# First transform with the matrix stationary, and its layout changed over HBM (FFT filter and top-1 mixture of experts, one core)

## The chip, the core and the metric

The program runs on one core of a Trainium2 chip. TensorE (PE) multiplies matrices and writes to PSUM, VectorE (DVE) and ScalarE (ACT) work element by element, GpSimd (POOL) does a part of that and issues indirect transfers, and SyncE (SP) issues the other DMA transfers; each engine executes its own instructions in the order in which the program put them there. The metric is the device time of one execution in microseconds, as the median of several.

## The reference: what is computed

```python
X = np.fft.rfft(x, axis=1)                    # x: 8 sequences x 2496 x 256
Y = X * (filt_r + 1j * filt_i)[None, :, :]
y = np.fft.irfft(Y, n=2496, axis=1)           # then 19968 rows of 256
expert_idx = np.argmax(y @ w_gate, axis=1)    # 8 experts
gate_w = softmax(y @ w_gate)[row, expert_idx]
out[row] = gate_w * (relu(y[row] @ w1[e]) @ w2[e])    # 256 -> 1024 -> 256
```

All of it is float32. The filter runs along the 2496 positions of a sequence, for each of 256 channels apart.

## The kernel before, in words

A sequence of 2496 positions is seen as 39 x 64 (position = 64 n1 + n2). The first transform goes along n1 (39 values become 39 real numbers: one constant, 19 cosines, 19 sines), the second along n2, with the twiddle factors in its matrices `bm`. Then come the product with the filter, the inverse along n2 (`cm`) into the tiles `U`, and the inverse along n1 (`dm`) together with the routing.

A *unit* u is one sequence and one half of its channels (128 of 256): 16 units. A unit has 5 *steps*, one for each group of four bins k, so t = 0 to 79. What a step t does, in the names of the functions:

- `forward1(u, j)`, six times for a unit: for up to four groups of three n2, the data `x` (117 rows of three n2 and 39 n1, 128 channels) are the stationary operand and the block matrix `a1` the moving one. The result in PSUM has channels on partitions; ACT, for one j DVE, copies it into `T` (lines 255 and 263).
- `spec1(t)`: four transposes of `T` (line 295) bring n2 to the partitions, and ACT copies the result to `z` (line 301).
- `spec2(t)`: eight products with `bm` (line 313); `filt_` and `join` (lines 330, 343 and 344) multiply by the filter and join the parts on DVE and POOL; `spec3(t)`: four products with `cm` (line 355), and ACT copies to `U` (line 360).

Beside the steps run the inverse of a sequence that is finished (`inv1` to `inv3`: transposes on line 622, products on line 648, copies on 629, 634 and 650, rows scattered to HBM by POOL on line 158), the routing (`route1` to `route6`) and the preparation of the experts' weights (`w_load` to `w_out`). All of these are put in one list with a key that is counted in steps, and the list is sorted by the key; this gives the order on every engine. From key 78 on the blocks of 128 rows go through the experts (lines 1030 and 1056); most of them run after the last step.

SP issues all plain transfers in the order of the list. A transfer that waits (for a free buffer, say) holds back what stands behind it on SP.

Of the kernel before, what the change touches and what calls it, by code (L numbers as in the profile page):

```python
# [22 lines left out]
N1, N2 = 39, 64  # L23
# [4 lines left out]
GP = 3 * N1  # L28
DUP = 18
# [9 lines left out]
def _dft_tables():  # L39
    n1, n2 = np.arange(N1), np.arange(N2)  # L40
    a = np.zeros((N1, N1))
# [72 lines left out]
def tile_fft_moe(ctx, tc, x, filt_r, filt_i, w_gate, w1, w2, cst, out):  # L114
# [22 lines left out]
    wscr = dram.tile([E, 128, 8256], F16, name="wscr")  # L137

# [46 lines left out]
    with ExitStack() as fctx:  # L185
# [3 lines left out]
        xp = pool(name="xp", bufs=3)  # L189
        up = pool(name="up", bufs=1)  # L190
        tp = pool(name="tp", bufs=1)
# [8 lines left out]
        sp = early(name="sp", bufs=2)  # L200
        pY = early(name="pY", bufs=3, space=PSUM)
# [4 lines left out]
        T = [tp.tile([128, N1, N2], F32, name=f"T{i}") for i in range(2)]  # L206
        a1 = fp.tile([GP, GP], F32, name="a1")
# [20 lines left out]
        xt = {}  # L228

        def loadx(u, c):  # L230
            b, h = divmod(u, 2)
            xv = x[b].rearrange("(n1 n2) d -> n1 n2 d", n2=N2)[
                :, :, h * 128 : (h + 1) * 128
            ]
            t = xp.tile([GP, 4, 128], F32, name=f"x{u}_{c}", tag="x", bufs=4)
            g0, g1 = BANKS[c]
            for l in range(3):
                n = min(g1, NG if l == 0 else NG - 1) - g0
                s0 = 3 * g0 + l
                nc.sync.dma_start(  # L240
                    t[l * N1 : (l + 1) * N1, :n, :],
                    xv[:, s0 : s0 + 3 * (n - 1) + 1 : 3, :],
                )
            for g in range(g0, g1):
                xt[u, g] = t[:, g - g0, :]

        BANKS = ((0, 4), (4, 8), (8, 12), (12, 16), (16, 20), (20, 22))

        def forward1(u, j):
            g0, g1 = BANKS[j]  # L250
            n = 0
            ps = pY.tile([128, 512], F32, name=f"f1_{u}_{j}", tag="pY")
            for g in range(g0, g1):
                m = GP if g < NG - 1 else N1
                nc.tensor.matmul(  # L255
                    ps[:, n : n + m],
                    lhsT=xt.pop((u, g))[:m],
                    rhs=a1[:m, :m],
                    start=True,
                    stop=True,  # L260
                )
                n += m
            (nc.scalar.copy if j in (0, 1, 2, 3, 5) else nc.vector.tensor_copy)(  # L263
                T[u % 2].rearrange("p r n -> p n r")[:, 3 * g0 : 3 * g0 + n // N1, :],
                ps[:, :n].rearrange("p (n r) -> p n r", r=N1),
            )
# [23 lines left out]
        def spec1(t):  # L290
            u, it = divmod(t, 5)
            ps = pA.tile([128, 4, 128], F32, name=f"pt{t}", tag="pF")
            for kk in range(4):
                o = max(0, 2 * (4 * it + kk) - 1) * 64
                nc.tensor.transpose(
                    ps[:, kk],
                    T[u % 2].rearrange("p r n -> p (r n)")[:, o : o + 128],
                    ident,
                )
            z = wp.tile([128, 4, 128], F32, name=f"z{t}", tag="z")  # L300
            nc.scalar.copy(z, ps)  # L301
            stk[t] = z

        def spec2(t):
            u, it = divmod(t, 5)
            z = stk[t]

            ps = pB.tile([128, 2, 2, 128], F32, name=f"px{t}", tag="pF")
            for j in range(2):
                for i in range(2):  # L310
                    for a in range(2):
# [4 lines left out]
                            rhs=z[:, kk],  # L316
# [5 lines left out]
        def filt_(t):  # L322
            u, it = divmod(t, 5)
            h = u % 2
# [22 lines left out]
        def spec3(t):  # L347
            u, it = divmod(t, 5)
# [3 lines left out]
            for kk in range(4):  # L352
# [8 lines left out]
                U[u % NU].rearrange("p n r -> p r n")[:, r0 : r0 + o // 64, :],  # L361
                ps[:, :o].rearrange("p (r n) -> p r n", n=N2),
# [390 lines left out]
        nc.gpsimd.dma_start(ident, cst["ident"])  # L753
        loadk(bm, "bm", 0, 1, nc.gpsimd)
        loadx(0, 0)
        loadx(0, 1)
        loadf(0)
        loadx(0, 2)
        loadx(0, 3)
        loadk(bm, "bm", 1, 2)  # L760
        loadk(cm, "cm", 0, 1)
# [6 lines left out]
        for j in range(6):  # L768
            forward1(0, j)
            if j < 2:  # L770
                loadx(0, j + 4)
# [50 lines left out]
        slow = lambda t: min(1.0, max(0.6, 1.0 - 0.06 * (t - 72)))  # L822
        for t in range(NT):
            u, it = divmod(t, 5)
            rho = slow(t)
            at(t, spec1, t)
# [4 lines left out]
            if 0 < t < 5:  # L831
                at(max(t - 1.8, 0.05), loadf, t)
            if u + 1 < NU_ALL and it == 0:
                for j in range(6):
                    at(t + K["f"] + K["fd"] * j if u else 1.6 + 0.55 * j, forward1, u + 1, j)
            if u + 1 < NU_ALL and it == 0:
                for j in range(6):

                    n = 6 * (u + 1) + j - 4
                    v, i = divmod(n, 6)  # L840
                    z = 5 * (v - 1) + K["f"] + K["fd"] * i + 0.02
                    if v < 2:
                        z = 1.6 + 0.55 * i + 0.02 if v else 0.2 + 0.25 * j
# [340 lines left out]
```

## Time and profile before

| | us |
|---|---|
| median of 3 executions (1471.96 to 1482.54) | 1473.03 |
| the profiled execution | 1473.7 |
| its span, first to last instruction | 1471.9 |

```profile
PE 1345.9 (91%) x15559; PEld 1207.6 (82%) x15559; DVE 879.7 (60%) x2550; ACT 846.7 (58%) x1440; POOL 485.7 (33%) x525
```

This is the first part of the profile's page: for each engine its busy time, the share of the span, and the instructions. PEld are the weight loads of TensorE, which overlap with its products. A share over the whole span is a mean over stages of different kinds: some 81 us of start, six sequences in a steady rhythm, the last steps, the last inverse and routing, and then the experts alone.

### The profile page before, as it was taken

How to read it: one execution, taken by the hardware profiler on the slowest of the kernel's cores; microseconds unless marked ns; L12 is line 12 of the kernel's file. 1: busy time of each engine (PE TensorE's matmuls, PEld its weight loads, DVE VectorE, ACT ScalarE, POOL GpSimd, SP SyncE). 2: the span in 40 equal slices, each digit the busy share in tenths (PEclk: the TensorE clock that was granted, in tenths of full speed). 3: DMA queues.
4: the chain of work that ended last, by engine and by line, in shares of the span. 5: the costliest groups of instructions: out<-in, count | busy, mean ns of one | idle time of the engine just before them, and what ended most of it. 6: DMA issues, size and time to landing. Idle time of an engine off the chain costs nothing.

```text
span 1471.9 us, 41507 instructions
## 1 busy us (share of the span) xinstructions
PE 1345.9 (91%) x15559; PEld 1207.6 (82%) x15559; DVE 879.7 (60%) x2550; ACT 846.7 (58%) x1440; POOL 485.7 (33%) x525
## 2 busy tenths in 40 slices
PE   6888888889989878689999999999999999999997
PEld 5767677777867667479999988999998998999997
DVE  1589788797987657245555554555555555555552
ACT  2547566566755455356666655665566565665564
POOL 1235665656656652432111111111111111111111
PEclk7899999999998999799999999999999999999999
DMA  5744544545543252249346369534535336434631
GB/s 165 210 154 158 163 145 162 176 157 176 165 143 98 73 179 59 84 127 271 73 107 163 81 154 338 158 78 106 155 77 155 104 77 174 91 77 105 157 75 44
DMA packets 200119, 199.18 MB, mean 135 GB/s; under 512 B 104707, under 2 KB 178100, under 8 KB 191724
## 3 DMA queue, kind: packets, MB, share of 16 engines
q1 hardware_dynamic: 180396, 153.80, 37.2%
q0 software_dynamic: 19520, 42.71, 10.4%
q8 instruction: 124, 2.03, 0.6%
q14 instruction: 79, 0.65, 0.1%
HBM read 347.54 MB, written 61.56 MB: 278 GB/s over the span
## 4 chain that ended last, share of the span: by engine, by line
PE 46%; DMA 4%; issue 2%; DVE 2%; SPq 1%; ACT 1%; POOL 0%; POOLq 0%; ACTq 0%; DVEq 0%
PE ph L1030 24%; PE po L1056 22%; DMA wa<-wscr 2%; DMA wb<-wscr 2%; DVE hl L1044 1%; SPq L939 1%; ACT hs L1036 0%; ACT hh L1038 0%; POOL out_dram L158 0%; DMA xt<-xs 0%; SPq L1017 0%; DVE m L995 0%; ACT xs L1009 0%; SPq L947 0%; SPq L977 0%
## 5 line engine op out<-in xcount | busy, mean ns | idle before, releaser
L1030 PE MATMUL ph<-xt,wa 128*128 128x128 f16 x7728 | 468.5, 221 | 24.8 <-DMA wa<-wscr 12.5
L1030 PEld LDWEIGHTS <-wa 128*128 128x128 f16 x7728 | 450.3, 99 | 37.3 <-issue 17.4
L1044 DVE TENSOR_TENSOR hl<-hs,hh 128x512 f16<-128x512 f32 x322 | 223.1, 693 | 376.0 <-ACT hh L1038 319.0
L1056 PE MATMUL po<-wb,hh 128*128 128x256 f16 x2576 | 432.9, 273 | 4.4 <-DMA wb<-wscr 2.1
L158 POOL DMA_INDIRECT out_dram<-ot,t x161 | 158.7, 986 | 693.9 <-DVE xs L1010 616.7
L1056 PE MATMUL po<-wb,hl 128*128 128x256 f16 x1288 | 351.6, 273 | 0.5 <-issue 0.4
L1056 PEld LDWEIGHTS <-hh 128*128 128x128 f16 x2576 | 245.4, 98 | 34.9 <-issue 5.8
L1036 ACT ACTIVATE hs<-ph 128x512 f32<-128x512 f32 x322 | 191.9, 596 | 108.6 <-PE ph L1030 98.3
L158 POOL DMA_INDIRECT xs<-yt,dest x176 | 184.4, 1048 | 132.1 <-issue 65.3
L1009 ACT ACTIVATE xs<-xb,s 128x256 f16<-128x256 f32 x161 | 82.0, 509 | 228.2 <-DVE s L999 226.7
L1038 ACT CAST hh<-hs 128x512 f16<-128x512 f32 x322 | 199.5, 620 | 10.3
L1056 PEld LDWEIGHTS <-hl 128*128 128x128 f16 x1288 | 126.2, 98 | 15.9 <-issue 1.1
L255 PE MATMUL f<-a,x 117*128 117x117 f32 x704 | 108.1, 298 | 16.8 <-DMA x<-in_x_dram 15.1
L360 ACT COPY U<-pi 128x512 f32<-128x512 f32 (+1 forms) x80 | 88.0, 1099 | 58.7 <-PE pi L355 56.4
L255 PEld LDWEIGHTS f<-a,x 117*128 117x128 f32 x704 | 98.2, 211 | 25.0 <-issue 16.0
L1010 DVE SCALAR_TENSOR_TENSOR xs<-xb,s,xs 128x256 f16<-128x256 f32 x161 | 78.3, 486 | 55.7 <-ACT xs L1009 52.9
L343 POOL TENSOR_TENSOR p<-tr,ti 64x256 f32<-64x256 f32 x80 | 65.4, 818 | 137.3 <-DVE ti L330 123.1
L355 PE MATMUL pi<-cm,p 128*128 128x128 f32 (+1 forms) x640 | 92.7, 289 | 11.6 <-POOL p L344 7.7
L355 PEld LDWEIGHTS pi<-cm,p 128*128 128x128 f32 x640 | 81.3, 197 | 22.4 <-issue 11.5
L263 ACT COPY T<-f 128x468 f32<-128x468 f32 (+1 forms) x80 | 71.2, 890 | 46.9 <-PE f L255 45.7
L313 PE MATMUL px<-z,bm 128*64 128x128 f32 x1280 | 92.5, 289 | 3.7 <-ACT z L301 2.1
L650 ACT COPY yt<-py 117x512 f32<-117x512 f32 x88 | 53.0, 603 | 61.4 <-PE py L648 34.8
(171 smaller groups left out, 1488.2 us busy)
## 6 DMA issues: line engine op xcount, KB each, us to landing
wb<-wscr SPq DMA_DIRECT2D x134, 1040.0 KB
wa<-wscr SPq DMA_DIRECT2D x134, 1024.0 KB
xb<-xs SPq DMA_DIRECT2D x161, 130.0 KB
x<-in_x_dram SPq DMA_DIRECT2D x240, 78.0 KB
wf<-in_moe_w_dram SPq DMA_DIRECT2D x32, 512.0 KB
wscr<-wh SPq DMA_DIRECT2D x8, 1040.0 KB
wscr<-wh SPq DMA_DIRECT2D x8, 1024.0 KB
xs<-yt,dest POOLq DMA_INDIRECT x176
```

The lines of the kernel that those rows point to most:

```text
L158: nc.gpsimd.indirect_dma_start(out=dst, out_offset=bass.IndirectOffsetOnAxis(ap=idx, axis=0), in_=src, in_offset=None, bounds_check=bound, ...
L255: nc.tensor.matmul(ps[:, n : n + m], lhsT=xt.pop((u, g))[:m], rhs=a1[:m, :m], start=True, stop=True,)
L313: nc.tensor.matmul(ps[64 * a : 64 * a + 64, i, j], lhsT=bm[:, 4 * it + kk, 64 * i : 64 * i + 64], rhs=z[:, kk], start=True, stop=True,)
L355: nc.tensor.matmul(ps[:, o : o + n], lhsT=p[:, kk], rhs=cm[:, k, :n], start=True, stop=True)
L360: nc.scalar.copy(U[u % NU].rearrange("p n r -> p r n")[:, r0 : r0 + o // 64, :], ps[:, :o].rearrange("p (r n) -> p r n", n=N2),)
L1009: nc.scalar.activation(xs_[:, 0], xb[:, :D], AF.Copy, scale=sc)
L1010: nc.vector.scalar_tensor_tensor(xs_[:, 1], xb[:, :D], sc, xs_[:, 0], op0=ALU.mult, op1=ALU.subtract)
L1030: nc.tensor.matmul(ps[:, f], lhsT=w[:, p : p + 128], rhs=xt[:, r, c], start=(n == 0), stop=(n == 5))
L1036: nc.scalar.activation(s, ps, AF.Relu, scale=1.0 / B23)
L1038: nc.scalar.copy(hh, s)
L1044: nc.vector.tensor_tensor(hl, s, hh, op=ALU.subtract)
L1056: nc.tensor.matmul(ps, lhsT=h2[q][:, f % 4], rhs=wv[:, r, f], start=(f == 0 and n == 0), stop=(f == 7 and n == 2),)
```

## The change: what it does

- The matrix `a1` is now the stationary operand of the first transform (117 x 120: three n2 at once, 40 rows for each, cosines ahead of sines) and the data the moving one, with two groups and all 256 channels at a time: 512 columns. There are 11 products for a sequence in place of 44, and 11 copies (ACT) into `y`.
- `y` goes to HBM (`fscr`), six transfers for a sequence, and comes back as `z` with n2 on the partitions: 30 transfers for a sequence, six for each group of bins. The transposes, `T` and the copies to `z` are gone.
- `x` is loaded for all 256 channels at once. The two halves of the channels take turns in the steps: t now counts sequence, group of bins, half. `z`, `bm` and the filter's group `ff` so serve two steps in a row.
- The copy to `U` writes runs of eight adjacent elements and reads PSUM with a stride; before it read adjacent elements and wrote with a stride.

```diff
-    a = np.zeros((N1, N1))
+    a = np.zeros((N1, 40))
-        a[:, 2 * k - 1], a[:, 2 * k] = np.cos(ph), -np.sin(ph)
+        a[:, k], a[:, 20 + k] = np.cos(ph), -np.sin(ph)
...
+    fscr = [dram.tile([FR, NG, D], F32, name=f"fscr{i}") for i in range(2)]
...
+        def loadx(b, c):
+            xv = x[b].rearrange("(n1 n2) d -> n1 n2 d", n2=N2)
+            t = xp.tile([GP, 4, D], F32, name=f"x{b}_{c}", tag="x")
+            n = min(4, NG - 4 * c)
+            for l in range(3 if n == 4 else 2):
+                o = NG * l + 4 * c
+                nc.sync.dma_start(
+                    t[l * N1 : (l + 1) * N1, :n, :], xv[:, o : o + n, :]
+                )
...
+        def forward1(b, j):
+            c, i = divmod(j, 2)
+            m, q = (GP, FR) if j < 10 else (2 * N1, 80)
+            ps = pY.tile([128, 512], F32, name=f"f1_{b}_{j}", tag="pY")
+            nc.tensor.matmul(
+                ps[:q],
+                lhsT=a1[:m, :q],
+                rhs=xt[b, c][:m, 2 * i : 2 * i + 2, :].rearrange("p g d -> p (g d)"),
...
+                yt1[b, c] = xp.tile([FR, 4, D], F32, name=f"y{b}_{c}", tag="y", bufs=2)
...
+                nc.sync.dma_start(fscr[b % 2][:q, 4 * c : 4 * c + n, :], y[:q, :n, :])
...
+        def loadz(b, it):
+            z = wp.tile([128, 4, D], F32, name=f"z{b}_{it}", tag="z", bufs=4)
             for l in range(3):
...
+                n = NG if l < 2 else N2 - 2 * NG
+                for a in range(2):
+                    o = 40 * l + 20 * a + 4 * it
+                    nc.sync.dma_start(
+                        z[64 * a + NG * l : 64 * a + NG * l + n],
+                        fscr[b % 2][o : o + 4, :n, :].rearrange("k g d -> g k d"),
+                    )
...
-                            rhs=z[:, kk],
+                            rhs=z[:, kk, h * 128 : h * 128 + 128],
...
-                U[u % NU].rearrange("p n r -> p r n")[:, r0 : r0 + o // 64, :],
-                ps[:, :o].rearrange("p (r n) -> p r n", n=N2),
+                U[u % NU][:, :, r0 : r0 + o // 64],
+                ps[:, :o].rearrange("p (r n) -> p n r", n=N2),
...
+        f1 = lambda b, j: 10 * (b - 1) + (0.3 + 0.6 * j if b > 1 else 1.5 + 0.5 * j)
```

Three places show how the order moves. The first is TensorE in the steady part, a stretch of about a step and a half: before, `pt` are the transposes, `f` the first transform, `px` and `pi` the products with `bm` and `cm`.

```order
L295 MATMUL pt_1877<-ident,T_108 128x128 x4
L313 MATMUL px_1889<-z_1803,bm 64x128 x8
L255 MATMUL f_6_2_1903<-a_109,x_2_1634 128x117 x4
L355 MATMUL pi_1913<-cm,p_1793 128x128 x4
L622 MATMUL pg_1_1919<-ident,U_123 117x128
...
L295 MATMUL pt_1936<-ident,T_108 128x128 x4
```

```order
L246 MATMUL f_3_3_1380<-x_1_878,a_106 120x512
L313 MATMUL px_1392<-z_0_1005,bm 64x128 x8
...
L354 MATMUL pi_1421<-cm,p_1294 128x128 x4
L621 MATMUL pg_9_1427<-ident,U_118 117x128
...
L246 MATMUL f_3_4_1450<-x_2_950,a_106 120x512
```

The transposes are gone, and single products of 512 columns stand where groups of four products of 117 columns stood.

The second is SP in the steady part, of the change alone; `fscr<-y` are the writes, `z<-fscr` the loads back, `wf` and `wscr` the experts' weights.

```order
L261 DMA fscr_59<-y_4_913 120x1024
L237 DMA x_2_950<-in_x_dram 39x1024 x3
L261 DMA fscr_59<-y_5_982 80x512
L237 DMA x_3_986<-in_x_dram 39x1024 x3
L271 DMA z_0_1005<-fscr_59 22x4x256 x4
L271 DMA z_0_1005<-fscr_59 20x4x256 x2
L271 DMA z_1_1012<-fscr_59 22x4x256 x4
L271 DMA z_1_1012<-fscr_59 20x4x256 x2
L470 DMA wscr<-wh_0_955 128x4096
```

Between the loads of `x` now stand the writes of `y`, and the first load of `z` stands behind the last write of its sequence, for which it waits.

The third is SP at the start, before and now.

```order
L240 DMA x_0_133<-in_x_dram 39x4x128 x3
L240 DMA x_1_137<-in_x_dram 39x4x128 x3
L280 DMA ff_125<-in_filt_r_dram 32x512
...
L286 DMA ff_125<-in_filt_i_dram 32x2x256
L240 DMA x_2_153<-in_x_dram 39x4x128 x3
L240 DMA x_3_157<-in_x_dram 39x4x128 x3
```

```order
L237 DMA x_3_140<-in_x_dram 39x1024 x3
...
L261 DMA fscr_59<-y_4_196 120x1024
L261 DMA fscr_59<-y_5_204 80x512
L271 DMA z_0_207<-fscr_59 22x4x256 x4
...
L271 DMA z_1_214<-fscr_59 20x4x256 x2
L289 DMA ff_122<-in_filt_r_dram 32x512
```

The filter's first group (`ff`) moved from behind the second load of `x` to behind all writes of the first sequence and two groups of loads of `z`.

## Rows read from the trace of the kernel before

**Rows 1.** Busy time in five stretches: from the start to the product with `bm` of step 10, six sequences of steps (10 to 69), the last ten steps, the last inverse and routing, the experts alone. Columns: stretch, its length, busy us of PE, PEld, DVE, ACT, POOL (instructions), granted TensorE clock as a share of 2.4 GHz, busy share of the 16 DMA engines, GB/s.

```profile
0.00:81.30 81.30, 58.64 (x433) 50.47 (x433) 35.70 (x59) 31.62 (x40) 17.80 (x30) 0.83 0.66 190
81.30:465.90 384.60, 341.95 (x2954) 284.61 (x2954) 323.68 (x697) 240.74 (x351) 226.94 (x246) 0.96 0.49 156
465.90:532.50 66.60, 52.27 (x431) 40.92 (x430) 40.56 (x104) 33.82 (x57) 47.98 (x54) 0.97 0.41 137
532.50:640.00 107.50, 85.81 (x881) 70.90 (x881) 50.46 (x193) 48.46 (x88) 39.35 (x42) 0.85 0.25 68
640.00:1472.00 832.00, 807.26 (x10866) 760.72 (x10863) 429.28 (x1498) 492.10 (x905) 153.64 (x156) 0.99 0.50 129
```

**Rows 2.** The timeline of TensorE where the products with `bm` of steps 0, 10, 70 and 79 begin (start, us, engine, line, operation).

```profile
21.93 1.66 PE L313 MATMUL px<-z,bm 128*64 128x128 f32 x16
...
81.32 0.48 PE L313 MATMUL px<-z,bm 128*64 128x128 f32 x2
...
465.90 0.33 PE L313 MATMUL px<-z,bm 128*64 128x128 f32 x2
...
532.51 0.48 PE L313 MATMUL px<-z,bm 128*64 128x128 f32 x2
```

**Rows 3.** The stretch of the six sequences again, for one line each: in this order line 255 (first transform; PE, PEld), line 295 (transposes; PE, PEld), line 263 (copies to `T`; DVE, ACT), line 301 (copies to `z`; ACT). Then line 255 and line 295 in the last ten steps.

```profile
81.30:465.90 384.60, 77.59 (x528) 70.48 (x528) 0.96 0.49 156
...
81.30:465.90 384.60, 39.54 (x241) 30.00 (x240) 0.96 0.49 156
...
81.30:465.90 384.60, 11.65 (x12) 53.67 (x60) 0.96 0.49 156
...
81.30:465.90 384.60, 35.35 (x60) 0.96 0.49 156
...
465.90:532.50 66.60, 3.96 (x28) 3.51 (x28) 0.97 0.41 137
...
465.90:532.50 66.60, 5.08 (x32) 3.53 (x32) 0.97 0.41 137
```

**Rows 4.** Groups of instructions by line and shape in the same 384.6 us: busy us, mean ns of one, idle time before them and what ended it. A plain float32 product is two instructions here.

```profile
L313 PE MATMUL px<-z,bm 128*64 128x128 f32 x960 | 67.9, 285 | 1.6 <-ACT z L301 1.2 <-DVE gq L634 0.4
...
L648 PE MATMUL py<-gh,dlo 117*117 117x512 f32 x61 | 24.8, 407 | 0.0
...
L486 PE MATMUL plw<-U,wg 128*32 128x351 f32 x192 | 18.5, 480 | 14.3 <-DVE gl L516 7.2 <-ACT U L360 6.3 <-issue 0.8
...
L360 ACT COPY U<-pi 128x512 f32<-128x512 f32 x48 | 54.0, 1125 | 24.9 <-PE pi L355 24.1 <-issue 0.7
...
L650 ACT COPY yt<-py 117x512 f32<-117x512 f32 x61 | 36.9, 605 | 39.2 <-PE py L648 30.2 <-PE pg L622 6.4 <-issue 1.2
...
L301 ACT COPY z<-pt 128x512 f32<-128x512 f32 x60 | 35.4, 589 | 7.9 <-PE pt L295 7.4
```

**Rows 5.** Who waited for whom in the same stretch (us in total, times, longest), of DVE and of SP's queue.

```profile
DVE tr L330 <- PE px L313: 16.9, 8, 3.6
...
DVE T L263 <- PE f L255: 9.8, 5, 4.1
...
SPq L240 <- PE f L255: 201.1, 53, 8.4
```

**Rows 6.** DMA queues in the same stretch: packets, MB, share of 16 engines' time.

```profile
q1 hardware_dynamic: 44044, 45.43, 36.7%
q0 software_dynamic: 7552, 13.97, 11.8%
```

**Rows 7.** Two shorter stretches, with the columns of rows 1: the one with the highest busy share of DVE, and one with the highest share of the DMA engines (the experts' weights begin to be loaded there).

```profile
100.00:150.00 50.00, 45.77 (x412) 39.57 (x411) 48.20 (x98) 34.42 (x49) 25.30 (x29) 1.00 0.49 157
...
650.00:700.00 50.00, 49.42 (x676) 46.65 (x674) 28.60 (x105) 30.44 (x58) 9.33 (x9) 1.00 0.93 248
```

**Rows 8.** The start: SP's issue of transfers of the filter's group, one of several alike, and the first product with the filter on DVE, which waited for that group.

```profile
19.17 0.42 SPq L280 DMA_DIRECT2D ff<-in_filt_i_dram  x1
...
23.64 0.69 DVE L330 TENSOR_TENSOR tr<-px,ff 128x512 f32<-128x512 f32 x1 [3.71 <-DMA ff<-in_filt_r_dram]
```

More of the change, by code (lines that the diff above doesn't have):

```diff
@@ L28 @@
 GP = 3 * N1
+FR = 120
 DUP = 18
@@ L205, in tile_fft_moe @@
         bm = kp.tile([128, 20, 128], F32, name="bm")
-        T = [tp.tile([128, N1, N2], F32, name=f"T{i}") for i in range(2)]
-        a1 = fp.tile([GP, GP], F32, name="a1")
+        a1 = fp.tile([GP, FR], F32, name="a1")
         dm = fp.tile([GP, GP], F32, name="dm")
@@ L247, in tile_fft_moe @@
[L247 to L266, printed above, removed]
+        yt1 = {}
@@ new lines, in loadx @@
+        def loadx(b, c):
[7 more added lines that the diff above has]
+                )
+            xt[b, c] = t
+        def forward1(b, j):
[6 more added lines that the diff above has]
+                rhs=xt[b, c][:m, 2 * i : 2 * i + 2, :].rearrange("p g d -> p (g d)"),
+                start=True,
+                stop=True,
+            )
+            if i == 0:
+                yt1[b, c] = xp.tile([FR, 4, D], F32, name=f"y{b}_{c}", tag="y", bufs=2)
+            y = yt1[b, c]
+            nc.scalar.copy(
+                y[:q, 2 * i : 2 * i + 2, :].rearrange("p g d -> p (g d)"), ps[:q]
+            )
+            if i == 1 or j == 10:
+                n = 2 * i + 2
+                nc.sync.dma_start(fscr[b % 2][:q, 4 * c : 4 * c + n, :], y[:q, :n, :])
@@ L288, in loadf, with place @@
                         )
[L290 to L302, printed above, removed]
+        def place(t):
+            b, k = divmod(t, 10)
+            it, h = divmod(k, 2)
+            return b, 2 * b + h, it, h
         def spec2(t):
-            u, it = divmod(t, 5)
-            z = stk[t]
+            b, u, it, h = place(t)
+            z = zt[b, it]
             ps = pB.tile([128, 2, 2, 128], F32, name=f"px{t}", tag="pF")
@@ L322, in filt_ @@
         def filt_(t):
-            u, it = divmod(t, 5)
-            h = u % 2
+            b, u, it, h = place(t)
             ps = stk[t]
@@ L347, in spec3 @@
         def spec3(t):
-            u, it = divmod(t, 5)
+            b, u, it, h = place(t)
             p = stk.pop(t)
@@ L752, in tile_fft_moe @@
         nc.gpsimd.dma_start(a1, cst["a1"])
-        nc.gpsimd.dma_start(ident, cst["ident"])
+        for c in range(4):
+            loadx(0, c)
         loadk(bm, "bm", 0, 1, nc.gpsimd)
[L755 to L761, printed above, removed]
         warm = wp.tile([128, 512], BF16, name="warm", tag="lw", bufs=1)
@@ L767, in tile_fft_moe @@
             nc.tensor.matmul(ps, lhsT=warm[:, :128], rhs=warm, start=True, stop=True)
-        for j in range(6):
+        for j in range(11):
             forward1(0, j)
-            if j < 2:
-                loadx(0, j + 4)
+            if j in (1, 3):
+                loadx(0, 4 + j // 2)
+        for it in range(2):
+            loadz(0, it)
+        loadf(0)
+        loadk(cm, "cm", 0, 1)
+        loadk(bm, "bm", 1, 2)
+        nc.gpsimd.dma_start(ident, cst["ident"])
         late = (dm, "dm"), (small, "small"), (zrow, "zrow"), (ids, "ids"), (dup, "dup")
```

55 lines of the change are left out of this document (21 added, 34 removed).

## The prediction

> **What bounds the kernel now.** I read the view of busy time in stretches first, then the timeline for the pace, then the groups by line inside the stretch that the change touches. The stretches [rows 1] show that the last 832 us are the experts alone, with TensorE busy 97%; the change touches nothing there. What the change can win lies ahead of 532.5 us. The products of steps 10 and 70 begin at 81.32 and 465.90 us [rows 2]: six sequences in 384.6 us, 64.1 us each. In these TensorE is busy 341.95 us (0.89), DVE 323.68 (0.84), ACT 240.74, POOL 226.94, and the DMA engines have a share of 0.49. So TensorE is nearest to its limit, and DVE stands close behind it. SP waited 201.1 us for the first transform to free a tile of `x` [rows 5]: transfers run ahead of the products, not behind them. In the waits DVE lost 16.9 us to the products with `bm` and 9.8 us to the first transform [rows 5]. The reader should see a chain of engines in fixed order, in which TensorE leads and DVE would be the next to lead.
>
> **The change part by part, for one sequence (a sixth of the 384.6 us).**
>
> *TensorE, off.* The first transform took 77.59 us and the transposes 39.54 [rows 3]: 12.9 and 6.6 us for a sequence.
>
> *TensorE, on.* 11 products of 512 float32 columns, two instructions each. No row has this shape, so I bound it. A column costs the difference between an instruction of 351 columns (480 ns) and one of 128 (285 ns) [rows 4], over 223 columns: 0.87 ns, so 448 ns for 512 columns, 0.90 us for a product and 9.9 us for 11. From below: an instruction of 512 columns of the inverse took 407 ns [rows 4], so 9.0 us. From above: the present transform's 77.59 us over 528 instructions of 117 columns [rows 3] is 147 ns, or 644 ns for 512 columns, 14.2 us. I take 9.9, because the rows that it comes from differ in columns and the high end includes a new stationary operand for every product, and that is what goes away. TensorE then has 57.0 - 12.9 - 6.6 + 9.9 = 47.4 us.
>
> *DVE.* It loses the copies to `T`: 11.65 us over six [rows 3], 1.9 for one. 53.9 becomes 52.0 us. DVE is now the fullest engine.
>
> *ACT.* Off: 53.67 and 35.35 us [rows 3], 14.8 for one. On: 11 copies at 605 ns (a 512-column copy out of PSUM [rows 4]), 6.7 us. The copy to `U` costs 1125 ns between 589, if the stride of its writes was the whole price, and 1125 if the stride of reads costs as much [rows 4]. Either way ACT falls from 40.1 to between 27 and 32 us for a sequence and is hidden behind DVE; I count nothing for it.
>
> *Transfers.* `y` is 5 x 120 x 4 KB and 80 x 2 KB, 2.62 MB; `z` is 5 x 128 x 4 KB, 2.62 MB. Now 59.4 MB took 48.5% of 384.6 us on all DMA engines [rows 6], 3.14 us for a MB. The 5.24 MB added cost 16.5 us, so the engines are busy 31.1 + 16.5 = 47.6 us for a sequence, still less than DVE. The packets of `x` grow from 512 bytes to 4 KB; what this saves I leave out. SP issues 17 + 6 + 30 transfers for `x`, `y` and `z` in place of 32, 21 more at 0.42 us [rows 8], 8.8 us in time that it now spends waiting [rows 5]. Each new wait on SP (a write for its copy, a load of `z` for the last write or for a free buffer) stands in key order; the loads of `z` are issued some five steps ahead of their use, nearly 30 us, and four tiles of `x` are as far ahead. So in the steady part these waits are covered; if the DMA engines became full that cover would be gone, which is the second rival.
>
> *The steady part.* DVE's 52.0 us set the period if waits allow. TensorE reached 0.89 in this stretch [rows 1], DVE reached 48.20 of 50 us, 0.96, at its fullest [rows 7]. I take 0.92, between the two, since the wait for the first transform is gone and TensorE, which feeds DVE, now has 4.6 us less to do than DVE. 52.0 / 0.92 = 56.5 us. Six sequences: 384.6 - 339 = **46 us saved**. Ends: 0.96 gives 54.2 and 59 us saved, 0.89 gives 58.4 and 34.
>
> *The last ten steps.* TensorE loses 4.0 + 5.1 us [rows 3] of 52.27, POOL keeps its 47.98 of 66.60 [rows 1]. No engine is full, so I take about half, **5 us saved**, between 0 and 9.
>
> *The start.* Up to step 10 the DMA engines are busy 0.66 of 81.3 us [rows 1], 53.7 us. Added by then are `y` of two sequences and `z` of the first and the first group of the second: 8.4 MB, 26.4 us. Together 80.1 us: at a share of 0.93, as in the fullest stretch shown [rows 7], 86 us, and at 0.89, 90. I take **9 us lost**. Besides, the first product with `bm`, at 21.93 us now [rows 2], needs the whole sequence transformed, written and read back, and the filter's group comes after that (12 issues of 0.42 us; DVE waited for that group already now, 3.71 us [rows 8]). Against it, a group of `ff` is now needed every second step. Ends: nothing lost, if the engines fill their gaps, and 20 us, if the round trip and the late filter stand in series with the steps.
>
> *The sum.* -46 - 5 + 9 = -42 us. The last inverse and the experts keep their time. The profiled execution took 1473.7 us with a span of 1471.9, the median is 1473.03; the difference is small, and I take the sum from the median: **1431 us**. The ends together: 1473 - 59 - 9 + 0 = 1405 and 1473 - 34 - 0 + 20 = 1459.
>
> **A rule against the change.** The trace gives one share for all 16 DMA engines, so 47.6 us is a mean. By it the transfers stay behind DVE. The Trainium skill, page "DMA: Bandwidth & Descriptors", section "Why a DMA increments its semaphore by 16 and not by 1", says that a transfer runs on as many engines, at most 16, as divide the outermost sizes of both sides, and on the lowest-numbered ones when SP issues it. By that rule, as an estimate, the loads of `z` with 22 and 20 rows would use 11 and 10 engines, those of `x` 13, the writes of `y` 15; the ten lowest would be busy 54.1 us for a sequence. No row of this case shows single engines.
>
> **The rivals.**
>
> *The transfers bind on a part of the engines.* If the added 2.62 MB of `z` lie on ten or eleven engines, each of these gets 12 of 128 rows, 0.246 MB at 50.2 us for a MB on one engine: 12.3 us; `y` adds 8.8 and the present `x` already lies 1.9 us above the mean: 31.1 + 12.3 + 8.8 + 1.9 = 54.1 us. This exceeds DVE's 52.0; at 0.92 the period is 58.8, 32 us saved: -32 - 5 + 9, **1445 us**. For it: small loads of 22 rows. Against: 512-byte packets of `x` go away. The rule above would give this case. Chance 0.18.
>
> *The transfers bind outright, and it gets slower.* If such a mix of transfers holds only a share of 0.70 (0.66 was reached at the start, while the steps waited for loads [rows 1]), the period is 47.6 / 0.70 = 68.0, 23 us lost over six, and the start takes 80.1 / 0.70 = 114, 33 lost: 23 + 33 - 5, **1524 us**. It decides as soon as the share that can be held falls below 47.6 / 64.1 = 0.74. Against it: 0.93 was held for 50 us [rows 7], with long packets. Chance 0.12.
>
> *The order, not TensorE, makes the rhythm.* If the fixed order keeps DVE at its present 0.84, the period is 52.0 / 0.842 = 61.8, 14 us saved, none at the end: -14 + 9, **1468 us**, no change that counts. For it: the keys were spaced for other costs, and the granted clock could fall with a less busy TensorE (0.96 in this stretch at a busy share of 0.89, 0.85 in 532.5 to 640 at 0.80 [rows 1]). Against: the largest wait of SP and one of DVE's end in the first transform [rows 5]. Chance 0.14.
>
> That the change does not do what it says is ruled out by the order that was shown: no transpose stands between `f` and `px`.
>
> **How the numbers follow.** The forecast of 1431 has the remaining 0.56, with 1405 to 1459 as its own range. The range of 1404 to 1474 takes in the first and third rival and leaves out the slower one, and a little on either side of the ends. About 1% is what a measurement of this kernel can tell from no change: 1458 and 1488. Faster: 0.54 of the forecast, 0.15 of the first rival, 0.01 of the third: 0.70. Within 1%: 0.02, 0.03 and 0.12: 0.17. Slower: 0.12 and 0.01: 0.13.
>
> **What would show it.** In the changed profile: the 11 products for a sequence at 9 to 10 us; DVE at 0.9 or more and TensorE near 0.84 between steps 10 and 70; a distance of 56 to 57 us between sequences; step 10 at about 90 us; a DMA share near 0.84. DVE below 0.87 with loads of `z` or `x` as releasers would speak for the first two rivals, with PE, ACT and DVE releasing each other for the third. The prediction is wrong if the experts' part changes its length, or if the start loses more than the steady part gains.

## The result and the profile after

The changed kernel took 1483.46 us in the median of 20 executions (1478.02 to 1490.86), the kernel before beside it 1473.72 (20 executions). The ratio is 1.0068, 95% interval 1.0051 to 1.0085: slower by 0.7%, where 1431 us and faster were forecast. The profiled execution took 1483.0 us with a span of 1481.2.

The same five stretches as in [rows 1], cut at the products with `bm` of steps 10, 70 and 79, with the same columns:

```profile
0.00:118.30 118.30, 55.97 (x287) 30.47 (x287) 33.42 (x56) 21.31 (x36) 18.07 (x30) 0.73 0.75 212
118.30:478.30 360.00, 314.64 (x2316) 221.05 (x2315) 311.83 (x682) 176.28 (x295) 219.15 (x241) 0.94 0.81 252
478.30:544.20 65.90, 48.18 (x371) 36.21 (x370) 42.59 (x108) 23.76 (x45) 52.90 (x59) 0.92 0.47 157
544.20:650.00 105.80, 83.94 (x867) 69.76 (x867) 49.68 (x193) 47.20 (x88) 38.36 (x40) 0.85 0.25 69
650.00:1481.00 831.00, 807.42 (x10880) 760.49 (x10877) 429.16 (x1498) 490.88 (x905) 154.24 (x157) 1.00 0.51 129
```

| stretch | before | after | difference | forecast |
|---|---|---|---|---|
| start, to step 10 | 81.3 | 118.3 | +37.0 | +9 |
| six sequences | 384.6 | 360.0 | -24.6 | -46 |
| last ten steps | 66.6 | 65.9 | -0.7 | -5 |
| all behind them | 939.4 | 937.0 | -2.4 | 0 |

The sum is +9.3 us. The start took more than the steady part gave. A sequence takes 60.0 us in place of 64.1; DVE works 311.83 / 6 = 52.0 us of it, TensorE 52.4.

The new product, line 246, in the same stretch alone (PE, PEld, clock, DMA share, GB/s):

```profile
118.30:478.30 360.00, 69.77 (x128) 19.23 (x128) 0.94 0.81 252
```

Groups by form in that stretch, which answer to [rows 4]: products with `bm`, copies to `y`, copies to `U`:

```profile
L313 PE MATMUL px<-z,bm 128*64 128x128 f32 x962 | 72.9, 298 | 9.4 <-issue 5.6 <-ACT U L359 3.7
...
L256 ACT COPY y<-f 120x512 f32<-120x512 f32 x58 | 34.0, 586 | 45.4 <-PE f L246 38.2 <-issue 4.4 <-PE px L313 1.7
...
L359 ACT COPY U<-pi 128x512 f32<-128x512 f32 x48 | 29.9, 624 | 58.3 <-PE pi L354 44.4 <-issue 10.4 <-PE f L246 2.5
```

The product takes 69.77 / 128 = 545 ns of TensorE for an instruction, a copy to `y` 586 ns. The copy to `U` fell from 1125 to 624 ns.

Who waited for whom in the start, up to step 10 (us in total, times, longest):

```profile
DVE tr L329 <- DMA ff<-in_filt_r_dram: 35.7, 1, 35.7
ACT y L256 <- DMA fscr<-y: 26.1, 6, 10.6
PE f L246 <- DMA x<-in_x_dram: 23.4, 3, 18.6
DVE wm L387 <- DMA wf<-in_moe_w_dram: 13.1, 3, 10.8
PE px L313 <- DMA z<-fscr: 10.1, 1, 10.1
```

Five different kinds of transfer are waited for. The first wait runs from the beginning, since DVE has no work before it; only some 3 us of it lie behind the first product with `bm`, which was done at 33.7 us while DVE began at 36.86. The same view for the six sequences, DVE and PE:

```profile
DVE tr L329 <- PE px L313: 19.1, 6, 4.4
DVE wh L458 <- ACT wh L453: 9.5, 11, 2.1
...
PE py L647 <- DVE gq L633: 10.9, 10, 2.1
PE pw L410 <- DVE wm L398: 9.7, 7, 2.7
```

No transfer stands among them (in the whole stretch PE and DVE never wait for one by this view, ACT for 1.0 us): the engines wait for each other. The timeline shows how, here at 250 us (the routing comes once in a sequence; TensorE, then DVE):

```profile
248.71 0.49 PE L503 MATMUL pgl<-ident,lw 128*117 128x128 f32 x3
249.04 1.02 PE L246 MATMUL f<-x,a 117*120 117x512 f32 x2
250.90 1.39 PE L485 MATMUL plw<-U,wg 128*32 128x351 f32 x16 [0.84 <-DVE gq L633]
252.22 0.70 PE L621 MATMUL pg<-ident,U 128*117 128x128 f32 x4
252.84 1.09 PE L313 MATMUL px<-z,bm 128*64 128x128 f32 x16
```

```profile
250.46 0.23 DVE L508 COPY gl<-pgl 117x72 f32<-117x72 f32 x1
250.60 0.15 DVE L515 COPY gl<-pgl 117x8 f32<-117x8 f32 x1
254.06 0.69 DVE L329 TENSOR_TENSOR tr<-px,ff 128x512 f32<-128x512 f32 x1 [3.30 <-PE px L313]
```

The routing has one PSUM buffer (`pD`). Its second group of products, `plw`, cannot begin before DVE has copied the first (`gl`, until 250.75; the view names `gq`, which DVE had done by 250.47), and `px` of the next step stands behind `plw` on TensorE. So DVE, having worked off its list, waits 3.30 us for `px`.

The start on TensorE (idle time before, and what ended it, in brackets):

```profile
31.77 1.97 PE L313 MATMUL px<-z,bm 128*64 128x128 f32 x16 [10.09 <-DMA z<-fscr]
52.36 3.46 PE L246 MATMUL f<-x,a 117*120 117x512 f32 x4 [18.62 <-DMA x<-in_x_dram]
70.15 2.06 PE L246 MATMUL f<-x,a 117*120 117x512 f32 x2 [4.60 <-ACT y L256]
82.29 2.06 PE L246 MATMUL f<-x,a 117*120 117x512 f32 x2 [5.33 <-ACT y L256]
117.75 0.59 PE L410 MATMUL pw<-ident,wm 128*1 128x128 f32 x2 [13.82 <-DVE wm L398]
118.27 1.97 PE L313 MATMUL px<-z,bm 128*64 128x128 f32 x16
```

### The profile page after: what moved, and what is told of

Its sections match the earlier page's. It is cut to its first block, busy times and chain, and to the rows that moved or that the text cites. A ratio compares the mean times of both kernels' runs of the same rounds, so it can differ in the third digit from the quotient of the medians.

```text
span 1481.2 us, 39900 instructions
## 1 busy us (share of the span) xinstructions
PE 1310.2 (88%) x14711; PEld 1118.0 (75%) x14711; DVE 866.7 (59%) x2534; ACT 759.4 (51%) x1368; POOL 482.7 (33%) x525
## 4 chain that ended last, share of the span: by engine, by line
PE 45%; DMA 5%; SPq 2%; issue 2%; DVE 1%; ACT 1%; POOL 0%; POOLq 0%; ACTq 0%; DVEq 0%
PE ph L1029 23%; PE po L1055 22%; DMA wb<-wscr 2%; DMA wa<-wscr 2%; SPq L938 1%; SPq L1016 1%; DVE hl L1043 1%; POOL out_dram L160 0%; DMA xt<-xs 0%; SPq L976 0%; ACT xs L1008 0%; ACT hs L1035 0%; SPq L946 0%; ACT hh L1037 0%; DVE xs L1009 0%
## 5 line engine op out<-in xcount | busy, mean ns | idle before, releaser
L246 PE MATMUL f<-x,a 117*120 117x512 f32 (+1 forms) x176 | 100.0, 662 | 39.4 <-DMA x<-in_x_dram 23.4
L313 PE MATMUL px<-z,bm 128*64 128x128 f32 x1280 | 99.2, 303 | 21.4 <-DMA z<-fscr 10.1
L256 ACT COPY y<-f 120x512 f32<-120x512 f32 (+1 forms) x88 | 51.3, 586 | 129.5 <-PE f L246 87.2
L313 PEld LDWEIGHTS px<-z,bm 128*64 128x64 f32 x1280 | 77.7, 150 | 52.7 <-issue 36.4
L354 PEld LDWEIGHTS pi<-cm,p 128*128 128x128 f32 x640 | 86.7, 206 | 35.9 <-POOL p L343 17.5
L354 PE MATMUL pi<-cm,p 128*128 128x128 f32 (+1 forms) x640 | 96.9, 298 | 15.4 <-POOL p L343 10.9
L329 DVE TENSOR_TENSOR tr<-px,ff 128x512 f32<-128x512 f32 x80 | 54.6, 683 | 86.9 <-PE px L313 40.5
L359 ACT COPY U<-pi 128x512 f32<-128x512 f32 (+1 forms) x80 | 49.0, 614 | 87.1 <-PE pi L354 68.4
```

The lines of the kernel that those rows point to most:

```text
L246: nc.tensor.matmul(ps[:q], lhsT=a1[:m, :q], rhs=xt[b, c][:m, 2 * i : 2 * i + 2, :].rearrange("p g d -> p (g d)"), start=True, stop=True,)
L313: nc.tensor.matmul(ps[64 * a : 64 * a + 64, i, j], lhsT=bm[:, 4 * it + kk, 64 * i : 64 * i + 64], rhs=z[:, kk, h * 128 : h * 128 + 128], s ...
L354: nc.tensor.matmul(ps[:, o : o + n], lhsT=p[:, kk], rhs=cm[:, k, :n], start=True, stop=True)
```

## The experiments

The kernel before took 1479.75, 1444.02, 1478.54, 1441.66 and 1481.45 us beside the five groups of runs (e1 to e4; e5 to e8; e9 to e12; e13 to e15; e16 to e18). Totals are compared inside a group only; the stages are read from the traces. "Step 10" is the start of its first product with `bm`, a sequence the sixth part of the time from there to step 70. Most runs were executed once, so a time of theirs is a single one. The groups differ behind step 79: 936 to 945 us in the first, third and fifth, 912 to 919 in the second and fourth; why is open. The six sequences hardly differ between the groups: where the products `f` and the routing's key stay as in the changed kernel or nearly so (e1 to e4, e7, e8, e10, e14 to e18), they took 59.4 to 60.6 us each. The start, where nothing in it was changed (e1, e2, e9, e18), reached step 10 at 116.7 to 119.5.

### Do the transfers bind the steady part?

**e1**: from the third sequence on no writes of `y` and no loads of `z`; the products use the second sequence's `z`.

```diff
-                nc.sync.dma_start(fscr[b % 2][:q, 4 * c : 4 * c + n, :], y[:q, :n, :])
+                if b < 2:
+                    nc.sync.dma_start(fscr[b % 2][:q, 4 * c : 4 * c + n, :], y[:q, :n, :])
...
+            if b > 1:
+                zt[b, it] = zt[1, it]
+                return
...
```

`z` gets a fifth buffer here, as all five tiles of the second sequence stay in use (in e6 and e13 too).

> From the third sequence on no y is written and no z loaded (the steps use the second sequence's z again, so the output is not the reference's from there on); all else of the change stays. In the changed kernel six sequences (steps 10 to 70) take 360.0 us, 60.0 each, with a DMA share of 0.81. Theory T, transfers bind the steady part: the DMA share falls to about 0.55 and the period to 57 or less, some 20 us less in all. Theory O, the fixed order makes TensorE and DVE take turns at being full inside a sequence, transfers are hidden: the period stays between 59 and 60.5, the time within 5 us of the changed kernel.

1479.46 us; step 10 at 117.5, step 70 at 475.7:

```profile
117.50:475.70 358.20, 315.03 (x2316) 221.83 (x2315) 313.79 (x683) 175.93 (x295) 221.91 (x242) 0.93 0.54 169
```

The DMA share falls from 0.81 to 0.54 and the sequence stays at 59.7 us. Transfers don't set it.

### What holds a sequence at 60 us?

**e2** spreads the products `f` over a sequence, **e4** moves those of the second sequence 1.5 steps later:

```diff
-        f1 = lambda b, j: 10 * (b - 1) + (0.3 + 0.6 * j if b > 1 else 1.5 + 0.5 * j)
+        f1 = lambda b, j: 10 * (b - 1) + (0.3 + 0.8 * j if b > 1 else 1.5 + 0.5 * j)
```

> The first transform's eleven products stand 0.8 steps apart in place of 0.6, so over 8 of 10 steps and not 6. Theory O: TensorE has less to do in the first six steps, where it is full, and more in the last four, where DVE is; the period falls from 60.0 to 57 to 58.5, 10 to 18 us less. Theory T: the same bytes in the same order, the period stays at 60 within 0.7, or grows, since z of the next sequence is loaded later.

1481.46 us, 59.8 us a sequence: the place of `f` in the sequence is not it.

```diff
-(0.3 + 0.6 * j if b > 1 else 1.5 + 0.5 * j)
+(0.3 + 0.6 * j if b > 1 else 3.0 + 0.55 * j)
```

> The first transform of the second sequence has keys 3.0 to 8.5 in place of 1.5 to 6.5; loads keep their order among themselves apart from what hangs on it. A theory P, that TensorE's order at the start costs most of the loss (its products for the second sequence wait 18.6 us for x, and step 1 stands behind them): step 1 moves from 55.8 to below 42, step 10 to 105 or less. Theories S and D: the steps start earlier but wait later for filter groups or z, step 10 stays within 6 us of 118.

1482.51 us. The products of step 1 (the second 16 of the first row) now begin at some 32.8 us, right behind those of step 0 and ahead of the wait for `x`, and step 10 begins at 116.2 (TensorE):

```profile
31.08 3.68 PE L313 MATMUL px<-z,bm 128*64 128x128 f32 x32 [10.14 <-DMA z<-fscr]
52.22 2.03 PE L246 MATMUL f<-x,a 117*120 117x512 f32 x2 [17.45 <-DMA x<-in_x_dram]
...
116.17 1.98 PE L313 MATMUL px<-z,bm 128*64 128x128 f32 x16 [10.41 <-DMA z<-fscr]
```

Step 1 came 23 us sooner, as Theory P has it, and step 10 hardly sooner, as S and D have it. The order of `f` and `px` in the start isn't what makes its end late; a sequence still takes 60.0 us.

**e6** leaves the first transform out from the third sequence on; **e9** moves one key; **e13** does both.

```diff
         def loadx(b, c):
+            if b > 1:
+                return
...
         def forward1(b, j):
+            if b > 1:
+                return
...
```

> From the third sequence on the first transform is left out (no loads of x, no products f, no copies and writes of y, no loads of z; the products with bm read the tiles of the second sequence). TensorE has 11.6 us less for a sequence, ACT 6.4 us less, DVE keeps its 52.0. Theory P (TensorE and DVE share the period, each full in turn, so what leaves TensorE shortens it): 54 to 57 us a sequence instead of 60.0. Theory R (the period is 52.0 of DVE and a fixed stretch at each sequence's beginning in which DVE waits for the routing and the inverse): 58 to 60.

1454.66 us. 59.9 us a sequence, with 11 products and 11 copies less (busy time from step 10 to step 70, then waits in it):

```profile
111.10:470.50 359.40, 280.75 (x2188) 216.76 (x2187) 314.52 (x682) 140.46 (x231) 222.36 (x241) 0.87 0.41 131
```

```profile
DVE tr L336 <- PE px L320: 25.4, 6, 5.9
...
PE plw L492 <- DVE gl L522: 17.2, 6, 4.2
```

TensorE's share falls to 0.78, yet DVE's wait for `px` grows to 4.2 us a sequence. The granted clock fell with it, from 0.94 to 0.87. By its numbers Theory R holds and P falls.

```diff
-        RT = (0.0, 0.4, 0.45, 0.9, 1.3, 1.7, 2.2, 2.5, 2.9, 3.3)
+        RT = (0.0, 0.4, 0.55, 0.9, 1.3, 1.7, 2.2, 2.5, 2.9, 3.3)
```

> The changed kernel with one key of the order moved: the routing's second group of products (plw) and what follows in its group stand 0.1 step later, so that the products px of the third step of a sequence stand ahead of them on TensorE. Theory R (DVE sets the period, and its longest wait is this: px stands on TensorE behind plw, plw waits until DVE has emptied the routing's only PSUM buffer, and DVE waits for px): the 3.2 us that DVE waits for px in a sequence go, 56.5 to 58 us a sequence, 10 to 20 us off the steady part, ratio to before 0.993 to 0.999. Theory M (the wait only moves to another pair of instructions): 59.5 to 60.5 us a sequence, ratio 1.004 to 1.009.

Ratio 1.004, interval 1.002 to 1.0061; 59.6 us a sequence. That is Theory M. DVE's wait for `px` did shrink, from 19.1 to 7.7 us over six sequences, and others came:

```profile
DVE tr L329 <- PE px L313: 7.7, 5, 2.5
DVE wh L458 <- ACT wh L453: 5.7, 9, 1.2
DVE rmx L535 <- PE pl L526: 5.1, 4, 2.9
DVE gl L508 <- PE pgl L503: 4.6, 5, 1.3
DVE tr L329 <- POOL p L343: 3.5, 2, 2.1
DVE wh L458 <- issue: 3.0, 3, 1.2
```

Taken alone, e6 excludes TensorE's load and e9 the order. So both were taken away:

> From the third sequence on no first transform, as in the experiment that left it out, and px ahead of the routing's second group, as in the one that moved it. Theory T (turns: in a sequence's first steps TensorE's order makes DVE wait, in the others TensorE's own work does, so that either alone leaves 60): 54 to 57 us a sequence. Theory V (DVE with what stands between its instructions needs 60 whatever TensorE does): 59 to 60.5. Left out: as in the experiment without the first transform.

1435.59 us:

```profile
111.00:450.00 339.00, 272.79 (x2188) 211.64 (x2187) 314.63 (x682) 140.90 (x231) 224.15 (x241) 0.89 0.43 139
```

```profile
DVE tr L336 <- PE px L320: 0.7, 1, 0.7
```

56.5 us a sequence, DVE at 0.928. Theory T holds: either limit alone keeps 60 us. In the same group e14 and e15, with both limits in place, took 59.7 and 59.4 us a sequence, so the group is not the reason; nor is the clock, which is lower in e13 (0.89) than there (0.95 and 0.94). In the changed kernel they lie in different steps of a sequence, as stretches of 6 us show (columns as in the first fence):

```profile
241.00:247.00 6.00, 5.97 (x53) 3.61 (x52) 4.74 (x11) 4.97 (x8) 4.90 (x5) 1.00 0.97 312
247.00:253.00 6.00, 5.16 (x36) 2.67 (x34) 3.67 (x8) 2.71 (x6) 5.26 (x7) 1.00 0.86 267
253.00:259.00 6.00, 6.00 (x53) 4.39 (x51) 4.87 (x10) 2.28 (x4) 5.01 (x6) 1.00 0.94 293
259.00:265.00 6.00, 6.00 (x44) 3.91 (x43) 5.42 (x17) 3.18 (x6) 2.65 (x3) 1.00 0.87 256
...
271.00:277.00 6.00, 3.71 (x34) 2.88 (x32) 5.77 (x12) 2.39 (x5) 4.22 (x5) 1.00 0.80 234
277.00:283.00 6.00, 4.19 (x34) 3.32 (x35) 5.82 (x13) 1.84 (x4) 1.71 (x2) 1.00 0.73 189
283.00:289.00 6.00, 4.33 (x40) 3.42 (x38) 5.86 (x14) 2.37 (x5) 2.99 (x3) 1.00 0.91 277
```

Around the routing and the inverse TensorE is full, or waits in that chain, and DVE has gaps; later DVE is full and TensorE has gaps.

### What does the start wait for?

**e3**: the filter, `bm`, `cm` and the constants are issued by POOL instead of SP, and the filter's first group earlier, right behind the first part of `bm`.

```diff
         def loadf(it):
+            nc_ = nc.gpsimd
-                    nc.sync.dma_start(t[q : q + 32, i], v[:, k : k + 2, :])
+                    nc_.dma_start(t[q : q + 32, i], v[:, k : k + 2, :])
...
-        def loadk(t, n, i0, i1, eng=nc.sync):
+        def loadk(t, n, i0, i1, eng=nc.gpsimd):
...
         loadk(bm, "bm", 0, 1, nc.gpsimd)
+        loadf(0)
...
-        loadf(0)
...
```

> The filter's groups, bm, cm and the small constants are issued by GpSimd in place of SP; the first filter group right after the first part of bm. Step 10 begins at 118.3 us in the changed kernel, 81.3 before. Theory S, the start is late because everything passes SP one after the other and x of the second sequence and the writes of y stand behind filter and constants: step 10 at 93 to 102, 16 to 25 us less in all. Theory D, the start is bound by the bytes that the DMA engines can move (25 MB by step 10): step 10 stays at 110 or later, the time within 8 us.

Step 10 at 106.2, between S and D: 12 us won with the same bytes (step 0, at 38.4, came 6.6 us later). Two things were moved at once, the issuing engine and the filter's first group, so not all of the 12 us need be SP's. The total was 1480.77, because this trace has 944.7 us behind step 79; why is not known.

**e7**: `x` of the second sequence ahead of the first `z`. **e8**: the weights' preparation later.

```diff
+        for c in range(4):
+            loadx(1, c)
         for it in range(2):
             loadz(0, it)
...
-(0.3 + 0.6 * j if b > 1 else 1.5 + 0.5 * j)
+(0.3 + 0.6 * j if b > 1 else 0.2 + 0.5 * j)
...
```

> In the start four groups of x of the second sequence are issued before the first loads of z, and the second sequence's products f stand 1.3 steps earlier in the order. Theory Q (SP's queue: the start is lost because x of the second sequence stands behind z, the filter and the constants): step 1 below 45 us, step 10 at 95 to 108. Theory D (the DMA engines are full, so the order of the transfers does not matter): step 0 two to four us later, step 10 at 115 to 122. Theory W (the end of the start hangs on the second weight tile, behind z on SP): step 10 at 113 to 118 with DVE waiting for wf.

1452.67 us. Step 1 at 44.0, as Q has it, but step 0 at 38.4 and step 10 at 115.6, as D and W have it: another order of the transfers moves the waits, not the end.

```diff
-        K = {..., "w": 6.0, "wp": 4.05}
+        K = {..., "w": 9.5, "wp": 4.05}
```

> The preparation of the experts' weights stands 3.5 steps later in the order, everything else as in the changed kernel. Theory W: in step 10 the wait of DVE for wf (10.8 us) goes and nothing replaces it: step 10 at 105 to 109. Theory Z (step 10 waits for its own z, whose loads wait for the last write of y): step 10 at 114 to 118, with z as releaser. The steady part, 59 to 61 us a sequence in both.

1461.66 us, step 10 at 110.6, between the two ranges, and DVE still waited 10.2 us for `wf` once: inconclusive. Up to there 22.3 MB were moved, 2.8 less than in the changed kernel, and the sequence behind it took 60.8 us in place of 56.8, so a part was only put off. (e6, with the weights in their place, has 111.1, but it leaves out 12 loads of `x` up to there.)

**e14** reads `z` of two sequences from the input, so no load waits for a write; **e15** also leaves out all writes of `y` and all loads of `z` but four tiles.

```diff
-                        fscr[b % 2][o : o + 4, :n, :].rearrange("k g d -> g k d"),
+                        (
+                            x[b].rearrange("(n1 n2) d -> n1 n2 d", n2=N2)[
+                                min(20 * a + 4 * it, 35) : min(20 * a + 4 * it, 35) + 4, NG * l : NG * l + n
+                            ]
+                            if b < 2
+                            else fscr[b % 2][o : o + 4, :n, :]
+                        ).rearrange("k g d -> g k d"),
```

> The changed kernel, but the tiles z of the first two sequences are read from the input x, in the same pieces and sizes, so that no load of z waits for a write of y; all writes of y stay (the first two sequences' spectra are wrong values of the right size). Theory L (latency: the round trip in series costs the start): step 0 at 20 to 26 us, step 10 at 85 to 100. Theory D (the bytes cost it, at the some 200 to 215 GB/s that every start so far moved): step 0 at 24 to 31, step 10 at 108 to 118.

1452.38 us; step 0 at 29.3, step 10 at 114.3. The wait for the write is not the price.

```diff
...
+            if b or it == 4:
+                zt[b, it] = zt[0, it % 4]
+                return
...
```

> The changed kernel without any write of y, and with four tiles of z in all, read once from the input x in the start and used by every step; the products f stay. The start moves 7.9 MB less than in the changed kernel, some 17 MB. Theory D: 17 MB at 200 to 215 GB/s, step 10 at 80 to 88 us. Theory S (SP's one queue, in which x of the second sequence stands behind 50 other transfers, costs it): step 10 at 92 to 108. The steady part as without the round trip, 59 to 60.5 us a sequence.

1423.92 us; step 10 at 89.1, just outside D's 80 to 88, since 18.28 MB were moved and not 17. Beside e14 in the same group that is 25 us sooner: the round trip's transfers are most of the 37 us. But e15 takes away transfers as well as bytes (141 issues of SP in place of 172). So one was added without the other, **e16** with transfers, **e17** with bytes, and **e18** is the changed kernel beside them:

```diff
+        def more(i):
+            for p in range(8 * i, 8 * i + 8):
+                nc.sync.dma_start(junk[p : p + 1], cst["small"][p : p + 1])
...
         def loadf(it):
+            if it:
+                more(it)
...
```

> The changed kernel with 40 more transfers of 256 bytes on SP's queue in the start, eight ahead of each group of the filter; nothing reads them. Theory I (SP's issue limits the start): 40 x 0.42 us = 17 us, so step 10 comes 10 to 17 us later than in the changed kernel on this chip. Theory D (the bytes limit it): 0 to 4 us later.

```diff
         loadf(0)
+        junk = dram.tile([S, D], F32, name="junk")
+        nc.sync.dma_start(junk, x[B - 1])
```

> The changed kernel with one more transfer of 2.56 MB in the start, HBM to HBM, behind the first group of the filter; nothing reads it. Theory D: at 3.8 us for a MB, the price between the kernel before and the changed one, step 10 comes 7 to 12 us later. Theory I: 0 to 4 us later, as the engines have gaps.

> The changed kernel itself, as the measure for the two others on this chip: step 10 at 114 to 120 us, 59.5 to 60.5 us a sequence.

The start up to step 10 in e16, e17 and e18:

```profile
0.00:131.00 131.00, 58.83 (x285) 32.14 (x285) 33.38 (x56) 21.15 (x36) 18.08 (x30) 0.72 0.68 192
```

```profile
0.00:128.10 128.10, 55.96 (x287) 30.30 (x287) 33.43 (x56) 21.19 (x36) 18.07 (x30) 0.73 0.76 219
```

```profile
0.00:116.70 116.70, 55.86 (x286) 30.17 (x286) 33.40 (x56) 21.23 (x36) 18.09 (x30) 0.77 0.76 215
```

40 tiny transfers cost 131.0 - 116.7 = 14.3 us, 0.36 us each (their own issues took SP 9.4 us), and 2.56 MB cost 11.4 us (4.5 us for a MB). Both are clear of the 2.8 us by which unchanged starts differ. Both theories hold, and neither excludes the other. But the two prices don't simply add: the change issues 32 transfers more up to step 10 and moves 9.7 MB more, which at these prices would be some 11 and 43 us, and it cost 37; for e15 they would give 43 where 25 were won. How issue and bytes overlap in the start is not shown. The totals point the same way: 1501.11 and 1490.79 against 1481.08.

| | step 10, us | MB moved till then | DMA share |
|---|---|---|---|
| before | 81.3 | 15.44 | 0.66 |
| e15, no round trip | 89.1 | 18.28 | 0.75 |
| e10 (below) | 96.5 | 19.29 | 0.70 |
| e3, POOL issues a part | 106.2 | 25.23 | 0.84 |
| changed | 118.3 | 25.12 | 0.75 |

SP's issues in the changed kernel up to step 10 sum to 75.7 us for 172 transfers; in the kernel before to 57.8 us for 140.

### The parts, and a faster version

**e5**: the kernel before with the new copy to `U` alone.

```diff
-                U[u % NU].rearrange("p n r -> p r n")[:, r0 : r0 + o // 64, :],
-                ps[:, :o].rearrange("p (r n) -> p r n", n=N2),
+                U[u % NU][:, :, r0 : r0 + o // 64],
+                ps[:, :o].rearrange("p (r n) -> p n r", n=N2),
```

> The kernel before, with one part of the change alone: the copy to U writes runs of eight. Theory H (hidden): ACT was busy 0.63 of the steady part, so a shorter copy moves nothing: 1469 to 1478 us, steps 10 to 70 in 383 to 386 us. Theory B (buffer): the copy also frees one of the four shared PSUM buffers 0.5 us sooner, ten times a sequence, and TensorE, busiest in this kernel, waits for those: 1455 to 1467 us, steps 10 to 70 in 372 to 380 us. The new copy is expected at 590 to 640 ns in both.

Ratio 0.9962, interval 0.9942 to 0.9982: a gain between the two theories, as 0.9962 of the 1473 us that they start from is 1467. The copy took 627 ns, a sequence 62.5 us, and the six together lie in Theory B's range:

```profile
79.90:455.00 375.10, 339.59 (x2954) 284.49 (x2953) 326.00 (x697) 219.30 (x352) 226.24 (x245) 0.96 0.50 160
```

These are 9.5 us less than in the trace of the kernel before, and the time is only 4.1 us less. That trace is not from this group, so how much the six sequences really gained is open.

**e12** is e5 with the key of e9 (`RT`, 0.45 to 0.55).

> The kernel before with the new copy to U and the same key moved. Theory R: DVE's waits for px (16.9 us over six sequences in the kernel before) shrink, but there DVE also waits for f, and TensorE is at 0.89: 1 to 2 us a sequence off the 62.5 of the kernel before with the new copy, ratio to before 0.988 to 0.993. Theory M: ratio 0.994 to 0.998, as with the new copy alone.

Ratio 0.988, interval 0.984 to 0.9921. A sequence takes 62.0 us, DVE's wait for `px` falls from 20.8 (e5) to 6.5 us over six. That is 0.5 us a sequence less than in e5, half of R's lower end, and within the 1.2 us by which steady parts differ from run to run. The ratio is better than that of e5, which is from another group, by more than these 3 us; where the rest comes from is open.

**e10** transforms the first sequence as before, the others as in the change; **e11** adds the key of e9.

```diff
+        T = [Uf[2 + i].rearrange("p (r n) -> p r n", n=N2) for i in range(2)]
...
+            if t < 10:
+                at(t, spec1, t)
...
-(0.3 + 0.6 * j if b > 1 else 1.5 + 0.5 * j)
+(0.3 + 0.6 * j if b > 1 else 4.2 + 0.42 * j)
```

> The first sequence alone is transformed as before the change (x stationary, transposes, halves one after the other, T in the place of two tiles of U that are not yet used); the other seven as in the changed kernel, their products f in the first sequence's steps 4 to 9. Theory A (the gain in the steady part and the loss at the start are independent): step 10 at 80 to 90 us, 59 to 61 us a sequence, ratio to before 0.976 to 0.988. Theory B (the bytes that the round trip adds are what costs, and they only shift): step 10 at 95 to 110 us or the first steady sequence at over 65 us, ratio 0.993 to 1.006.

Ratio 0.9901, interval 0.9872 to 0.993; step 10 at 96.5, 60.6 us a sequence: between A and B. 22 of the 37 us come back; with the other 15 go 3.9 MB and 9 issues of SP more than in the kernel before.

> The two edits before together. If both R and A hold, their gains add: step 10 at 80 to 90 us, 56.5 to 58 us a sequence, ratio to before 0.968 to 0.980. If M holds, as with the first sequence's old way alone.

Ratio 0.9885, interval 0.9845 to 0.9924; 94.6 us, then 59.5 a sequence. e10, e11 and e12 are about 1% faster than the kernel before beside them, which the changed kernel is not. e12 gets there without the new transform.

## Why the prediction was wrong, point by point

**The start: +9 forecast, +37 measured.** The step that failed is the one from busy time to time: "80.1 us: at a share of 0.93 ... 86 us, and at 0.89, 90". The engines kept 0.75. They were busy 0.75 x 118.3 = 88.7 us, since 25.12 MB were moved, 9.7 more than before and not 8.4 (eight groups of `z` were loaded by then, not six). At a share of 0.93 these 88.7 us would have put step 10 at 95; it came at 118, so most of the miss is the share, with no row behind it that the start could hold one of 0.89 or more (it held 0.66 [rows 1]). I counted 21 more issues by SP for a sequence and hid them in time in which SP waits. In the steady part e1 bears that out; in the start SP waited some 25 us of 118.3 and issued for 75.7, and e16 shows 40 more issues to delay step 10 by 14.3 us. The Trainium skill, page "DMA: Bandwidth & Descriptors", section "Issuing engines are not separate DMA queues", says that issuing from several engines only saves the sequencer's time, usually small beside the transfer itself. In e3, where POOL issued a part, 12 us were saved, the filter's earlier first group included; here that is not small. This term is 28 of the 52 us by which the forecast missed. The end "20 us" for it was too near, too.

**The steady part: -46 forecast, -24.6 measured.** DVE's 52.0 us were right to the decimal. The share was not: 0.92 assumed, 0.866 measured. The reason given was that TensorE "now has 4.6 us less to do than DVE". It has 0.4 us more: 52.4 in place of 47.4. Of the 5.0 us the product `f` explains 1.7 (69.77 / 6 = 11.6 for 9.9; 545 ns inside the ends of 407 and 644), the other products 3.3 (`px` 298 ns in place of 285; the granted clock was 0.94 of 2.4 GHz, 0.96 before; how much of it is the clock is open). The forecast 448 ns for an instruction of `f` took only the slope of its two rows, 0.87 ns a column, and left out the 173 ns that the same rows give besides; with them it would be 621 ns. With TensorE relieved and the wait behind `plw` gone, e13 does reach 0.928 and 56.5 us, with 272.79 / 6 = 45.5 us for TensorE, so the step would hold for a kernel that this is not.

**The third rival was nearest for the steady part**: 61.8 us a sequence by the order alone, 60.0 measured. It had 0.14, and gave 1468 because it shared the start's +9. Its mechanism is half of what the runs show: e6 and e13 show that the order holds the rhythm once TensorE is relieved, and e9 that with `f` in place the order alone does not.

**The first two rivals fall in the steady part.** The share of 0.81 is near the forecast 0.84, and without the round trip (e1) nothing changes. But the second rival's price for the start, 33 us at a share of 0.70, was the right size (partly by luck: the share was 0.75, and the engines had 88.7 us to do, not 80.1); the error was to tie it to a steady share below 0.74. The two have separate conditions. The first rival's terms for a part of the engines (8.8 us for `y`, 1.9 for `x`) can't be seen in any run, since each trace has one share for all 16; e1 shows only that no transfer set the period.

**Right**: ACT is hidden (176.28 / 6 = 29.4 us, between 27 and 32), the copy to `U` lies near its lower end (624 ns), the experts keep their time. The last ten steps gave 0.7 us in place of 5, near the lower end. The text named the case that came: "if the start loses more than the steady part gains".

## What to carry to other kernels

A transfer that is hidden in the steady part can be in series at the start: price the start by itself, with the number of issues on the one queue and the bytes, and don't fill the gaps of the DMA engines on paper. When an engine is relieved, look in the order for the wait that is next: two limits in different steps of a period each look innocent when only one is removed, so remove both before either is ruled out. Two cheap edits (a copy's stride and one key, e12) won about 1%, as much as the large one with its start mended (e11).

## What the runs showed of the hardware

A plain transfer issued by SP takes 0.42 us of its queue [rows 8]; 40 of 256 bytes each took it 9.4 us and delayed the start by 14.3 us (e16). Leaving out the products `f` (e6) lowered TensorE's share from 0.87 to 0.78 and the granted clock, a mean over the stretch, from 0.94 to 0.87 of 2.4 GHz (0.94 in e7 and e8 of the same group), and the products that stayed took 280.75 / 6 = 46.8 us a sequence, where 52.4 - 11.6 = 40.8 were left. How much of the 6.0 us is the clock was not separated.
